# Thirty small DMAs of 1 to 15 rows beside the loads of a one-core attention and gated-MLP decode kernel

## The chip, the cores and the metric

The kernel runs on one NeuronCore of a Trainium2 chip. The metric is the device time of one execution in microseconds. The kernel before took 196.21 us (median of two runs, 196.06 and 196.36). A third execution, taken under the profiler, is the one that every view of the profile below describes.

## The reference

```
W = min(4096, max(256, Sk // 4))                         # 4096 of 16384 cached positions
q = (x @ wq) -> [4 batches, 32 heads, 1, 128]
k = repeat(k_cache[:, :, Sk - W:, :], 4); v the same     # 8 cached heads, 4 query heads to each
p = softmax(q k^T * 128 ** -0.5);  a = (p v) @ wo
gate, up = x @ W_gate, x @ W_up                          # 512 -> 1792
b = (gate * (gate > 0) * up) @ W_down
g = sigmoid(sum(x * gate_w))
out = g * a + (1 - g) * b                                # [4, 1, 512], bf16
```

One token per batch attends to 4096 cached positions of 8 heads. A gated MLP of the same token is mixed in by a scalar gate. Almost all of the work is moving bytes: K and V come to 67 MB, the weights to 14 MB.

## The kernel before

The cache is cut into eight sets (`NSET`), each one half of the heads of one batch. A set's K is one DMA of 4 MB into a half of `Ksb`, and its V one DMA of 4 MB into a half of `Vsb`; both tensors have two halves, so two sets are on the chip at a time. `load_k` (L238) and `load_v` (L242) issue them. The K of set s may be issued when the scores of set s - 2 are done with the half (the event `("SC", s - 2, 3)`), the V when the products of set s - 2 are (`("PV", s - 2, 3)`).

Every large load is issued by SP (SyncE), in the order of the code, on SP's one queue. SP executes in order: a DMA that waits for its event holds up everything behind it. The order is WQ (L248), K of set 0, then for s = 1 to 7 the pair K of s and V of s - 1, then W_gate and W_up (L253, L255) into the half of `Ksb` that is free by then, V of set 7, W_down (L258), and wo in three column pieces (L264) and two last pieces of 128 KB (L267). The output goes out at L600. Only two tiny loads, x of four rows and gate_w of one row, are issued by ACT (L246, L247).

TensorE transposes the K of a set as fp32 pairs into PSUM (L346); ACT and DVE copy the result back over K (L351, L353); TensorE makes scores (L379); DVE masks them and takes maxima (L387); ACT takes exponentials (L416); DVE transposes them (L423); TensorE multiplies with V (L435). The sets s are pipelined: the K of set s is worked on while the softmax and the V product of set s - 1 run. After set 7 come the MLP, and the products with W_down and wo, which add up in one PSUM bank (L572). The very last ones wait for the last 128 KB piece of wo.

Every instruction is recorded in a `Program`, which gives each event a semaphore. `Program.dma` gives each DMA without a slot a semaphore of its own, and a landed DMA adds 16 to it. The last entry of SP's list is a bare wait, emitted behind the block's closing barrier:

```
P.dma("sp", lambda e: e.dma_start(out.rearrange("b o d -> (b o) d"), outs[:, :]), ("OUT",), [("OUTS", 3)])
P.op("sp", None, None, [("OUT",)])
```

Of the kernel before, what the change touches and what calls it, by code (L numbers as in the profile page):

```python
# [6 lines left out]
BF16 = mybir.dt.bfloat16  # L7
# [147 lines left out]
def bass_gated_mix__sliding_block_cached__glu_gated_reglu__decode_kernel(  # L155
# [13 lines left out]
    with ExitStack() as ctx:  # L169
        def sb(name, shape, dt):  # L170
            return ctx.enter_context(nc.sbuf_tensor(name, shape, dt))
# [36 lines left out]
        gtmp2 = sb("gtmp2", [128, NFT, 32], FP32)  # L208
        gtmp3 = sb("gtmp3", [128, NFT, 32], FP32)
        hT = sb("hT", [128, NFT, 32], BF16)  # L210
        outs = sb("outs", [4, 512], BF16)
        banks = [ctx.enter_context(nc.psum_tensor("bank%d" % i, [128, 512], FP32)) for i in range(8)]
        TR = banks[0:NTR]
# [10 lines left out]
        P = Program()  # L224
# [9 lines left out]
        def heads(cache, s):  # L234
            b, half = s // 2, s % 2
            return cache[b, 4 * half:4 * half + 4, SK - WIN:SK, :].rearrange("h (r c) d -> r h (c d)", r=32)

        def load_k(s):  # L238
            P.dma("sp", lambda e: e.dma_start(Ksb[:, s % 2, :], heads(A_k_cache, s)), ("K", s),
                  [("SC", s - 2, NBANK - 1)] if s >= 2 else [], slot="k%d" % (s % 2))  # L240

        def load_v(s):  # L242
            P.dma("sp", lambda e: e.dma_start(Vsb[:, s % 2, :], heads(A_v_cache, s)), ("V", s),
                  [("PV", s - 2, 3)] if s >= 2 else [], slot="v%d" % (s % 2))
# [2 lines left out]
        P.dma("act", lambda e: e.dma_start(xsb[4:5, :], gate_w.rearrange("(o d) -> o d", o=1)), ("GW",))  # L247
        P.dma("sp", lambda e: e.dma_start(Wbig[:, :], A_wq.rearrange("(p t) w -> p (t w)", p=128)), ("WQ",))  # L248
        load_k(0)
        for s in range(1, NSET):  # L250
            load_k(s)
            load_v(s - 1)
        P.dma("sp", lambda e: e.dma_start(Ksb[:, 0, 0:4 * FF], B_W_gate.rearrange("(p t) f -> p (t f)", p=128)),  # L253
              ("WG",), [("SC", NSET - 2, NBANK - 1)])
        P.dma("sp", lambda e: e.dma_start(Ksb[:, 0, 4 * FF:8 * FF], B_W_up.rearrange("(p t) f -> p (t f)", p=128)),  # L255
              ("WU",), [("SC", NSET - 2, NBANK - 1)])
        load_v(NSET - 1)
        P.dma("sp", lambda e: e.dma_start(Vsb[:, 0, 0:NFT * 512], B_W_down.rearrange("(p i) w -> p (i w)", p=128)),  # L258
              ("WD",), [("PV", NSET - 2, 3)])
        wo_src = A_wo.rearrange("(p i) w -> p (i w)", p=128)  # L260
# [337 lines left out]
            else:  # L598
                P.op(engine, lambda e, to=to, src=src: e.tensor_copy(to, src), ("OUTS", g), [("ACC", g)])  # L599
        P.dma("sp", lambda e: e.dma_start(out.rearrange("b o d -> (b o) d"), outs[:, :]), ("OUT",), [("OUTS", 3)])  # L600
        P.op("sp", None, None, [("OUT",)])

        sems = {name: ctx.enter_context(nc.semaphore(name)) for name in P.sems}
        P.emit("sp", nc.sync, sems, 0, 1)
# [50 lines left out]
```

## Time and profile before

| what | value |
|---|---|
| median of the two runs | 196.21 us |
| the profiled execution: its time | 196.31 us |
| its span, first to last instruction | 195.07 us |
| granted TensorE clock, mean | 0.913 |
| PE, DVE, ACT busy | 72%, 55%, 48% of the span |
| POOL busy | 4% of the span |
| instructions of the program on SP | 31 |
| HBM read | 81.01 MB |
| bytes of all DMA packets | 81.17 MB |

The profiled execution took 196.31 us, of which 195.07 us are its span; the 1.24 us around the span are outside the program's own instructions. The page gives the busy time of each engine, and the busy share of the core's 16 DMA engines in 40 slices of the span. The chain of waits is followed back from the last instruction to what released each step. SP's row of the timeline gives the start and the duration of every DMA issue; a gap in it is SP waiting. The page's list of DMA queues gives packets: one packet is what one DMA engine moves in one piece, and each has a start, a duration and a size in the trace. On the queue of the large loads the packets are 32 KB for WQ, K and V, less for the later weights, and 4 bytes for each step that a DMA engine adds to a semaphore. Packets marked "instruction" bring program code.

### The profile page before, as it was taken

How to read it: one execution, taken by the hardware profiler on the slowest of the kernel's cores; microseconds unless marked ns; L12 is line 12 of the kernel's file. 1: busy time of each engine (PE TensorE's matmuls, PEld its weight loads, DVE VectorE, ACT ScalarE, POOL GpSimd, SP SyncE). 2: the span in 40 equal slices, each digit the busy share in tenths (PEclk: the TensorE clock that was granted, in tenths of full speed). 3: DMA queues.
4: the chain of work that ended last, by engine and by line, in shares of the span. 5: the costliest groups of instructions: out<-in, count | busy, mean ns of one | idle time of the engine just before them, and what ended most of it. 6: DMA issues, size and time to landing. Idle time of an engine off the chain costs nothing.

```text
span 195.1 us, 3974 instructions
## 1 busy us (share of the span) xinstructions
PE 139.6 (72%) x1710; PEld 99.7 (51%) x1710; DVE 106.5 (55%) x283; ACT 93.3 (48%) x112; POOL 7.4 (4%) x37
## 2 busy tenths in 40 slices
PE   0135399789499929992999399939992999708665
PEld 0012385446287518751966296628751775404423
DVE  2104055986649455945485648574955595790201
ACT  2002188797088508760786087708860976220001
POOL 7300000000000000000000000000000000000000
PEclk9999999999979996997599859996999699996997
DMA  6999999999999999999999999999999999998992
GB/s 216 430 437 437 430 430 447 430 437 445 440 437 427 437 420 430 425 427 430 430 430 430 430 430 432 430 437 437 430 430 430 437 388 423 472 437 378 431 400 93
DMA packets 3885, 81.17 MB, mean 416 GB/s; under 512 B 409, under 2 KB 930, under 8 KB 1058
## 3 DMA queue, kind: packets, MB, share of 16 engines
q1 hardware_dynamic: 3864, 81.01, 97.2%
q8 instruction: 8, 0.13, 0.3%
q14 instruction: 3, 0.02, 0.0%
q10 hardware_dynamic: 10, 0.01, 0.0%
HBM read 81.01 MB, written 0.00 MB: 415 GB/s over the span
## 4 chain that ended last, share of the span: by engine, by line
DMA 58%; PE 29%; ACT 9%; DVE 1%; issue 1%; SPq 1%
DMA Ksb<-in_A_k_cache_dram 46%; PE bank L346 18%; DMA Wbig<-in_A_wo_dram 12%; ACT Ksb L351 7%; PE bank L379 6%; PE bank L435 2%; PE bank L448 2%; DVE Ksb L353 1%; ACT sc L416 1%; PE bank L572 1%; ACT L416 1%; SPq L264 0%; SPq L248 0%; SPq L258 0%; PE bank L451 0%
## 5 line engine op out<-in xcount | busy, mean ns | idle before, releaser
L346 PE MATMUL bank<-identf,Ksb 128*128 128x128 f32 x512 | 81.6, 314 | 27.4 <-DMA Ksb<-in_A_k_cache_dram 23.4
L351 ACT ACTIVATE Ksb<-bank 128x1024 bf16<-128x1024 bf16 x72 | 71.0, 1023 | 59.4 <-PE bank L346 59.0
L346 PEld LDWEIGHTS bank<-identf,Ksb 128*128 128x128 f32 x512 | 66.8, 161 | 42.1 <-DMA Ksb<-in_A_k_cache_dram 25.2
L353 DVE COPY Ksb<-bank 128x1024 bf16<-128x1024 bf16 x56 | 38.1, 685 | 40.3 <-PE bank L346 39.1
L387 DVE CUSTOM_DVE_ANT_0 sc<-bank,mask 128x512 bf16<-128x512 f32 x32 | 21.7, 686 | 9.7 <-PE bank L379 9.6
L379 PE MATMUL bank<-Ksb,QSP 128*32 128x512 bf16 x256 | 19.8, 390 | 2.2 <-DVE Ksb L353 1.6
L416 ACT ACTIVATE sc<-sc,negmax 128x1024 bf16<-128x1024 bf16 x16 | 18.3, 1145 | 4.8 <-DVE negmax L408 4.7
L423 DVE STREAM_TRANSPOSE pT<-sc 128x1024 bf16<-128x1024 bf16 x16 | 19.7, 1236 | 1.4 <-ACT sc L416 1.2
L435 PE MATMUL bank<-Vsb,pT 128*32 128x256 bf16 x512 | 19.2, 273 | 0.5 <-DMA Vsb<-in_A_v_cache_dram 0.5
L435 PEld LDWEIGHTS bank<-Vsb,pT 128*32 128x32 bf16 x512 | 12.2, 95 | 7.1 <-issue 3.8
L597 ACT ACTIVATE outs<-bank 4x128 bf16<-4x128 f32 x2 | 0.5, 270 | 21.2 <-PE bank L572 21.2
L448 PEld LDWEIGHTS bank<-osb,Wsel 128*64 128x64 f32 x128 | 8.1, 138 | 4.7 <-issue 2.9
L448 PE MATMUL bank<-osb,Wsel 128*64 128x32 f32 x128 | 9.0, 224 | 1.2 <-DVE osb L440 1.2
L516 PE MATMUL bank<-gwB,ident 128*128 128x512 bf16 x14 | 5.4, 535 | 5.4 <-DVE hT L509 5.4
L379 PEld LDWEIGHTS bank<-Ksb,QSP 128*32 128x32 bf16 x256 | 4.1, 94 | 9.6 <-DVE Ksb L353 4.1
L363 POOL COPY QSP<-QS 128x64 bf16<-128x64 bf16 x8 | 1.8, 238 | 119.7 <-PE bank L379 107.6
L440 DVE COPY osb<-bank 128x256 f32<-128x256 f32 x8 | 3.4, 421 | 5.4 <-PE bank L435 5.4
L465 PE MATMUL bank<-Wbig,xP 128*32 128x512 bf16 x32 | 3.6, 631 | 3.6 <-DMA Wbig<-in_A_wq_dram 3.6
L310 PE MATMUL bank<-ident,xsb 5*128 5x5 bf16 x4 | 0.3, 167 | 8.0 <-DMA xsb<-in_gate_w_dram 8.0
L599 DVE CAST outs<-bank 4x128 bf16<-4x128 f32 x2 | 0.6, 282 | 9.6 <-PE bank L572 9.6
L516 PEld LDWEIGHTS bank<-gwB,ident 128*128 128x128 bf16 x14 | 1.4, 118 | 7.7 <-DVE hT L509 5.8
L408 DVE TENSOR_SCALAR negmax<-mall 32x1 f32<-32x1 f32 x32 | 4.6, 144 | 1.0
(61 smaller groups left out, 55.9 us busy)
## 6 DMA issues: line engine op xcount, KB each, us to landing
Ksb<-in_A_k_cache_dram SPq DMA_DIRECT2D x8, 4096.0 KB, 22.7
Vsb<-in_A_v_cache_dram SPq DMA_DIRECT2D x8, 4096.0 KB, 31.9
Wbig<-in_A_wq_dram SPq DMA_DIRECT2D x1, 4096.0 KB, 12.1
Wbig<-in_A_wo_dram SPq DMA_DIRECT2D x1, 2048.0 KB, 20.8
Ksb<-in_B_W_gate_dram SPq DMA_DIRECT2D x1, 1792.0 KB, 18.0
Ksb<-in_B_W_up_dram SPq DMA_DIRECT2D x1, 1792.0 KB, 21.9
Vsb<-in_B_W_down_dram SPq DMA_DIRECT2D x1, 1792.0 KB, 16.3
Wbig<-in_A_wo_dram SPq DMA_DIRECT2D x1, 1280.0 KB, 23.5
```

The costliest lines, as they stand in the source:

```text
L346: P.op("pe", lambda e, bk=bk, cc=cc, c=c, s=s: e.transpose(bk[:, cc * 128:(cc + 1) * 128], kw[:, c * 128:(c + 1) * 128], identf[:, :]), (" ...
L351: P.op("act", lambda e: e.activation(dst, bk[:, :].bitcast(BF16), ACTF.Copy), ("KTC", s, i), [("KT", s, i)])
L353: P.op("dve", lambda e: e.tensor_copy(dst, bk[:, :].bitcast(BF16)), ("KTC", s, i), [("KT", s, i)])
L379: P.op("pe", lambda e, a=a, h=h: e.matmul(bk[32 * a:32 * a + 32, 0:512], QSP[:, s % 2, h, :], k4[:, 16 * bank:16 * bank + 16, 32 * a:32 * ...
L387: P.op("dve", lambda e: e.tensor_tensor_reduce(sc[:, s % 2, bank * 512:(bank + 1) * 512], bk[:, :], mask[:, :], 1.0, LOWEST, ALU.add, ALU.max,
L408: P.op("dve", lambda e, a=a: e.tensor_scalar(negmax[32 * a:32 * a + 32, par:par + 1], mall[:, 0:1], -SCALE, None, op0=ALU.mult), ("NEGMAX" ...
L416: P.op("act", lambda e: e.activation(sc[:, par, k * PW:(k + 1) * PW], sc[:, par, k * PW:(k + 1) * PW], ACTF.Exp, bias=negmax[:, par:par + ...
L423: P.op("dve", lambda e: e.transpose(pT[:, par, k * PW:(k + 1) * PW], sc[:, par, k * PW:(k + 1) * PW]), ("PTT", s, k), [("EXP", s, k), ("PV ...
L435: P.op("pe", lambda e, c=c, g=g, col=col: e.matmul(OB[32 * g:32 * g + 32, 0:256], pT[:, par, col:col + 32], v3[:, 16 * k + c, :], start=(k ...
L448: P.op("pe", lambda e, k=k, lo=lo: e.matmul(FB[r, 256:288], Wsel[:, lo:lo + 64], osb[:, par, 32 * k:32 * k + 32], start=(k == 0), stop=(k ...
L465: P.op("pe", lambda e, n=n, t=t, g=g, j=j: e.matmul(SCB[n][32 * g:32 * g + 32, 0:512], xP[:, t, :], Wq3[:, t, 512 * j:512 * j + 512], star ...
L516: P.op("pe", lambda e: e.matmul(TR[2][:, :], ident[:, :], gwB[:, :], start=True, stop=True), None, waits)
```

## The change

A scratch tensor `probe` is added, 16 partitions of 15 x 2 x 128 bf16 numbers. A function `ask(n, size)` issues 15 DMAs from SP; the k-th moves k rows of 4k + `size` numbers from the first rows of W_gate into `probe`. It is called twice: with size 64 behind the V of set 2, in the loop over the sets (rows of 136 to 248 bytes), and with size 0 behind the V of set 7 (rows of 8 to 120 bytes). No DMA of the two sets waits for anything, nothing reads `probe`, and each of the 30 has a semaphore of its own. The bare wait at the end of SP's list takes in all 30 besides the output's; as it is built, that is 16 semaphore instructions of one or two waits each where there was one, and the output's wait is in the last of them. Nothing changes on the other engines.

```diff
+        probe = sb("probe", [16, 15, 2, 128], BF16)
...
+        def ask(n, size):
+            for k in range(1, 16):
+                P.dma("sp", lambda e, k=k: e.dma_start(probe[0:k, k - 1, n, 0:4 * k + size], B_W_gate[0:k, 0:4 * k + size]),
+                      ("PROBE", n, k))
+
         for s in range(1, NSET):
             load_k(s)
             load_v(s - 1)
+            if s == 3:
+                ask(0, 64)
...
         load_v(NSET - 1)
+        ask(1, 0)
         P.dma("sp", lambda e: e.dma_start(Vsb[:, 0, 0:NFT * 512], B_W_down.rearrange("(p i) w -> p (i w)", p=128)),
               ("WD",), [("PV", NSET - 2, 3)])
...
-        P.op("sp", None, None, [("OUT",)])
+        P.op("sp", None, None, [("PROBE", n, k) for n in range(2) for k in range(1, 16)] + [("OUT",)])
```

## The prediction, made before the changed kernel ran

> **What bounds the kernel now.** First the page's slices, for the DMA engines.
>
> ```profile
> DMA  6999999999999999999999999999999999998992
> GB/s 216 430 437 437 430 430 447 430 437 445 440 437 427 437 420 430 425 427 430 430 430 430 430 430 432 430 437 437 430 430 430 437 388 423 472 437 378 431 400 93
> ...
> q1 hardware_dynamic: 3864, 81.01, 97.2%
> ...
> q14 instruction: 3, 0.02, 0.0%
> ```
>
> From the second slice to the last but three the 16 DMA engines never fall under nine tenths. SP's queue q1 alone fills 97.2% of their span. The kernel is a stream of bytes, and what lengthens the time is what takes DMA time, or what comes behind the stream. Second, the chain of waits over the end:
>
> ```profile
> 167.66 23.46 DMA Wbig<-in_A_wo_dram
> 191.12 0.04 issue
> 191.17 1.91 PE bank L572 x54
> 193.07 0.04 issue
> ```
>
> The last products wait for wo from 167.66 on; in the semaphore records the very last piece lands at 193.07, and 2.0 us of products, copies, output and closing follow. Third, SP's timeline, around the places of the two new sets:
>
> ```profile
> 51.15 0.60 SPq L243 DMA_DIRECT2D Vsb<-in_A_v_cache_dram  x1
> 68.51 0.54 SPq L239 DMA_DIRECT2D Ksb<-in_A_k_cache_dram  x1
> ...
> 147.68 0.55 SPq L243 DMA_DIRECT2D Vsb<-in_A_v_cache_dram  x1
> 166.82 0.33 SPq L258 DMA_DIRECT2D Vsb<-in_B_W_down_dram  x1
> ```
>
> SP idles 16.8 us (51.75 to 68.51) behind the V of set 2, and 18.6 us (148.23 to 166.82) behind the last V. Fourth, the DMA engines alone from 186 us on (40 slices of 0.23 us):
>
> ```profile
> DMA  7986979799799989989966455545000000000000
> ...
> DMA packets 842, 2.10 MB, mean 234 GB/s; under 512 B 76, under 2 KB 592, under 8 KB 720
> ```
>
> The engines do not finish together: from slice 20 (190.6 us) half of them are idle. The 16 steps of the last load's semaphore say it exactly: seven come at 190.91 to 191.19, one at 191.60, seven at 192.37 to 192.67, one at 193.07. The end is set by one DMA engine, 0.40 us behind the next and 2.16 us behind the first. The cause is in the packets: after one 16 KB instruction packet at 31.85, the V of set 0 has 15 steps at 41.70 to 42.04 and one at 43.52.
>
> **The new issues on SP.** One issue takes 0.23 us (gate_w's one row on ACT) to 0.56 us (x's four rows), and 0.04 to 0.06 us lie between two. Fifteen take 4.1 to 9.3 us and end inside SP's 16.8 and 18.6 us. The K of set 4 is queued behind the first set; were the cover gone, it would be issued late, which first costs when q1 runs dry, and the V ahead of it lands only at 80.6 to 82.4. W_down and wo are queued behind the second set; they are issued at 166.8 to 169.6, with the last V landing at 176.6 to 178.8. SP's issues: 0.
>
> **The new packets.** A DMA of k rows makes k packets on k DMA engines and k steps of 4 bytes: x's four rows left four packets and four steps, gate_w's one row one and one. That is 120 packets and 120 steps a set, 0 to 15 of each on an engine. The nearest rows: 512 B takes 27 ns and the next starts 23.5 ns later; 88 B (instruction queue) 9 ns; a 4 B step 9 ns. I take 13 ns for rows of 136 to 248 B (on the line from 88 to 512 B), 9 ns for the second set's 8 to 120 B, and 9 ns a step: 22 + 18 = 40 ns for one of each set. The trace does not show how many fall on the DMA engine that ends last. Half, eight of each set, are 0.32 us. The lower bound is 0 (it gets none). The upper is 15 x 2 x (27 + 9) = 1.08 us. If it gets none and the next one gets all, the end still moves by 0.60 - 0.40 = 0.20. I take 0.32.
>
> The Trainium skill, page "DMA: Bandwidth & Descriptors", section "Why a DMA increments its semaphore by 16 and not by 1", says that such a DMA takes the lowest-numbered k engines, so the first gets 15 of each set and the last none; no view here numbers the engines. By the same page's "Anatomy of one DMA" each DMA has a fixed cost of about 2.0 us (fitted for another issue path); 30 in a row would be 60 us by it, an estimate, against two loads of 128 KB at the end that land 0.36 to 0.40 us apart.
>
> A large packet behind tiny ones may start cold: the first 32 KB packets took 1.59 to 2.15 us, later ones 1.22, so at most 0.93 us a set, 1.9 us in all. No row has a large packet behind small ones. From 16 KB to 512 B packets nothing is lost at a change, so I take 0 and keep 1.9 for the range.
>
> **The new waits.** The 16 semaphore instructions at the end replace one. Now SP leaves the closing barrier at 194.49, and its last wait is recorded at 195.05, because the output's steps come until 195.03. That 0.56 us covers part of the 15 more. SP has no two of them in a row. From SP's own 17 ns of one and the 42 ns between its issues I get 59 ns from one to the next; POOL's pair at the barrier is 78 ns apart, PE's 150 ns. The last starts at 194.49 + 16 x 0.059 = 195.43, 0.38 us later than now; with POOL's 195.74 (+0.69); with PE's 196.89 (+1.84); with 17 ns they hide (0). I take SP's: 0.38. Without the cover it would be 15 x 0.059 = 0.89.
>
> **Sum.** 0 + 0.32 + 0.38 = 0.70. Span 195.07 + 0.70 = 195.77; 1.24 lies around the span, so 197.01. The profiled execution is 0.10 above the median of the runs, so 196.9. The change can hardly gain: even if all DMA engines ended with the first, only 2.16 us would go.
>
> **Rival 1: one more instruction packet.** The three 8 KB packets of q14 come at 44.0, 79.0 and 121.4. By then DVE had started 51 instructions, ACT 52, and DVE 187; POOL, with 47 in all, has none. So an engine seems to get one around its 52nd. SP goes from 31 to 76; its 52nd would be the first wo load, about 167 us. What one costs its DMA engine: 0.5 us (the step at 191.60 fits ACT's one) to 1.0 us (193.07 fits two of DVE's, 2.0 behind). On one of the seven early engines it is hidden; on the last it adds 0.5 to 1.0; on one of the seven late ones 1.0 - 0.40 = 0.6 at most. Time: 197.4 to 197.9. That it comes is likely; that it moves the end by 0.5 or more I give 0.20.
>
> **Rival 2: slower. Each tiny DMA holds its engine until its step is written.** Place: q1 of the first DMA engines, twice 15 steps in a row. Price: from a packet's start to the step seen, 0.36 us (x: 1.76 to 2.12) to 0.45 (192.62 to 193.07). 30 x 0.36 to 0.45 = 10.8 to 13.5 us, less the engine's lead of 0 to 2.16, and 0.38 of waits: 205.2 to 210.1. It makes over 2% from about 0.12 us a DMA (3.9 - 0.38 = 3.5, over 30), or 0.19 with the full lead. For it: no row has steps so close together. Against it: in this slice of the last engine's final packets,
>
> ```profile
> GB/s 0 52 0 0 51 0 51 0 51 0 0 51 0 51 0 51 0 0 51 0 51 0 51 0 0 51 0 51 0 51 0 0 51 0 51 0 0 0 0 0
> DMA packets 17, 0.01 MB, mean 19 GB/s; under 512 B 2, under 2 KB 17, under 8 KB 17
> ```
>
> (192.25 to 192.65) the step of the last load but one is at 192.263, and the next 512 B packet starts at 192.267: 4 ns. Chance 0.06. The page named above, "Queues, rings and completion order", says that a step is written only after every earlier write of its engine; the 4 ns show that the queue does not stand still for that.
>
> **Rival 3: nothing to see.** The late engine gets few of the rows, and SP's semaphore instructions follow at about their own 17 ns, so the output covers them. For it: the rows above leave both open. Against it: POOL and PE take three to five times as long between two as one lasts. Time 196.2 to 196.4. Chance 0.12.
>
> **How the numbers follow.** The forecast has 0.62; its own range is 196.5 (0.2 of packets, few waits shown) to 197.6 (waits by POOL's 0.69 and packets by 0.7). Rivals 0.20, 0.06 and 0.12. The range from 196.2 to 198.2 holds the forecast, rivals 1 and 3, and half of the cold starts; outside are rival 2, the full 1.9 us and PE's pitch together. About 2% (192.3 to 200.1) is what a measurement of this kernel is taken to tell from no change. Faster by that 0.01 (the 2.16 us above are less than 3.9), slower 0.07 (rival 2, and the upper bounds all at once, 196.2 + 1.08 + 1.9 + 1.84 = 201.0), within 0.92.
>
> **What would show it.** SP's timeline: 15 issues behind each of the two Vs, done before 61 and 158 us, the next K and W_down still at about 68.5 and 166.8. Landing steps: the last piece of wo up to 1 us after 193.07, the groups of its 16 steps spread by how many tiny packets each engine got. Packets: tiny ones 10 to 25 ns apart; hundreds of ns would be rival 2. A fourth 8 KB instruction packet near 167 us is rival 1. The end: 16 semaphore instructions on SP some 59 ns apart behind the barrier. I am wrong if the landing of V of set 2 moves by more than 1 us, if q1 shows a gap, or if the end moves by more than the two terms.

## The result, and the profile after

The changed kernel took 199.64 us (median of two runs, 199.57 and 199.72) against 196.21 us: a ratio of 1.0174, 95% interval 1.0158 to 1.0191. It is 3.4 us slower, 1.7%. The forecast was 196.9 us with a range up to 198.2, so the time fell outside it.

The profiled execution took 199.72 us with a span of 198.4 us. The page of the changed kernel, slices of the DMA engines and packets:

```profile
DMA  6999999999999999999999999999999999999981
...
DMA packets 4365, 81.21 MB, mean 409 GB/s; under 512 B 889, under 2 KB 1410, under 8 KB 1538
...
q1 hardware_dynamic: 4344, 81.04, 96.5%
```

The line of packets of the kernel before was:

```profile
DMA packets 3885, 81.17 MB, mean 416 GB/s; under 512 B 409, under 2 KB 930, under 8 KB 1058
```

There are 480 more packets under 512 B than before (889 against 409): the 240 rows and the 240 steps of their semaphores. The stream of bytes has no gap; it is longer. SP's timeline, around the two sets (start, duration, both in us):

```profile
52.33 0.72 SPq L244 DMA_DIRECT2D Vsb<-in_A_v_cache_dram  x1
53.09 5.44 SPq L253 DMA_DIRECT2D probe<-in_B_W_gate_dram  x15
68.49 0.55 SPq L240 DMA_DIRECT2D Ksb<-in_A_k_cache_dram  x1
...
150.43 5.40 SPq L253 DMA_DIRECT2D probe<-in_B_W_gate_dram  x15
169.28 0.35 SPq L267 DMA_DIRECT2D Vsb<-in_B_W_down_dram  x1
169.68 1.38 SPq L273 DMA_DIRECT2D Wbig<-in_A_wo_dram  x3
171.09 4.41 SPq L276 DMA_DIRECT2D Wbig<-in_A_wo_dram  x2
```

Fifteen issues take 5.4 us, inside SP's idle time as forecast; the next K goes out at 68.49, as before (68.51). The chain of waits at the end:

```profile
174.25 21.57 DMA Wbig<-in_A_wo_dram
195.82 0.04 issue
195.86 0.44 PE bank L581 x4
196.31 0.02 issue
196.33 0.27 ACT outs L606
```

The last piece of wo lands at 195.82 instead of 193.07: 2.75 of the 3.41 us between the two profiled executions. The rest, from the semaphore records: the output lands 2.06 us behind that piece (1.96 before), SP's last wait follows 0.48 us later (0.02 before), and 1.34 us lie around the span (1.24 before): 2.75 + 0.10 + 0.46 + 0.10 = 3.41. The DMA engines alone, from 186 us on (40 slices of 0.33 us):

```profile
DMA  9999999997998997798554333213000000000000
```

The engines end between 191.21 (the first step of the last load's semaphore) and 195.82 (the last): a spread of 4.6 us, where it was 2.16. The first is only 0.30 later than before. So the loss is not in all engines alike; some fell far back.

**What held them back.** The first DMA engine takes a packet and a step of each of the 15 DMAs. In the semaphore records of the changed kernel, the steps of the first set that follow each other on that engine come at 80.74, 80.91, 81.09, 81.28, 81.46, 81.66 and so on: 0.17 to 0.20 us apart, though each packet started 18 ns behind the one before. Their data and steps all started by 80.32; the 32 KB packet that started behind them at 80.33 took 2.58 us instead of 1.21. The reading from this, called theory S below: the steps of one DMA engine are written about 0.18 us apart, and a long run of them holds up the large packets behind it. Since the k-th DMA uses k engines, the trace also shows which engine is which: an engine that takes part from the k-th DMA on takes 16 - k of a set. The first step of the second set tells how late each engine was by then (us, relative to the engine that had five steps in the first set; those that had also fetched code are left out):

```
steps in the first set   15    13    11    9     8     7     6     5
lag at the second set    1.55  1.27  1.06  0.95  0.60  0.46  0.07  0
```

Several of the expectations below are worked out from this table: they take a run of n steps to cost n x 0.185 - 1.2 us, so that some six steps are free and fifteen cost 1.5 to 1.6 us. But the engines did not stand level at the first set, and the table leaves that out. A better measure is the time from an engine's first step of the first set to its first step of the second, less the 96.00 us between the first landings of the same two Vs in the kernel before (V of set 2 at 80.55, V of set 7 at 176.55). What the first set cost each engine (us):

```
steps   15    14    13    11    9     8     7     6     5     4     3     2     1
lost    2.00  1.92  1.64  1.41  1.13  1.04  0.46  0.23  0.12  0.10  0.07  0.04  0.03
```

Up to five steps in a row cost 0.12 us or less, six cost 0.23, and fifteen cost 2.0, not 1.55. Two engines are left out: the one with 12 steps lost 2.45 and the one with 10 lost 2.88, and between the two sets one 8 KB and one 16 KB code packet came, which are taken to be theirs.

The engine that ends last can be followed in the same records: its first step of the second set comes with the fourth DMA (180.32), the last at 182.37, the latest of the fifteen that take part. So it is the fourth engine, with 12 of each set. The second ends next. The fourth's loss can be added up: about 1.5 us for the first set, between the 1.41 of 11 steps and the 1.64 of 13, and 1.4 for the second, where its last V step and its W_down step are 5.71 us apart (180.15 and 185.86) against 4.30 before (178.82 and 183.12). This estimate of 2.9 us is near the 2.75 by which the last piece of wo is late.

### The profile page after: what moved, and what is told of

Same layout as the page of the kernel before. It is cut to its first block, busy times and chain, and to the rows that moved or that the text cites. A ratio compares the mean times of both kernels' runs of the same rounds, so it can differ in the third digit from the quotient of the medians.

```text
span 198.4 us, 4016 instructions
## 1 busy us (share of the span) xinstructions
PE 138.2 (70%) x1707; PEld 99.0 (50%) x1710; DVE 106.7 (54%) x283; ACT 93.1 (47%) x112; POOL 7.4 (4%) x37
## 4 chain that ended last, share of the span: by engine, by line
DMA 57%; PE 27%; ACT 8%; DVE 3%; SPq 3%; issue 1%
DMA Ksb<-in_A_k_cache_dram 46%; PE bank L355 17%; DMA Wbig<-in_A_wo_dram 11%; ACT Ksb L360 6%; PE bank L388 5%; PE bank L444 2%; DVE Ksb L362 2%; PE bank L457 2%; SPq L276 2%; ACT sc L425 1%; SPq L273 1%; ACT L425 1%; DVE pT L432 1%; DVE sc L396 0%; PE bank L581 0%
## 5 line engine op out<-in xcount | busy, mean ns | idle before, releaser
L444 PE MATMUL bank<-Vsb,pT 128*32 128x256 bf16 x512 | 19.8, 280 | 0.0
L525 PE MATMUL bank<-gwB,ident 128*128 128x512 bf16 x11 | 4.0, 495 | 6.1 <-DVE hT L518 5.8
L581 PE MATMUL bank<-Wbig,oq 128*32 128x128 bf16 x128 | 2.9, 223 | 4.4 <-DMA Wbig<-in_A_wo_dram 4.4
```

The lines of the kernel that those rows point to most:

```text
L444: P.op("pe", lambda e, c=c, g=g, col=col: e.matmul(OB[32 * g:32 * g + 32, 0:256], pT[:, par, col:col + 32], v3[:, 16 * k + c, :], start=(k ...
L525: P.op("pe", lambda e: e.matmul(TR[2][:, :], ident[:, :], gwB[:, :], start=True, stop=True), None, waits)
```

## The experiments

Each experiment is the changed kernel with the edit shown. Its last wait names the DMAs that it has. The landing of the last piece of wo, from the semaphore records, is called the last piece: 193.07 in the kernel before, 195.82 in the changed one. The ratios are against runs of the kernel before on the same chip, whose medians were 196.24 to 196.34 us.

**Packets kept, steps taken away.**

```diff
-            for k in range(1, 16):
-                P.dma("sp", lambda e, k=k: e.dma_start(probe[0:k, k - 1, n, 0:4 * k + size], B_W_gate[0:k, 0:4 * k + size]),
-                      ("PROBE", n, k))
+            w = 92 if n == 0 else 32
+            rows = B_W_gate[0:15, 0:15 * 112].rearrange("p (k w) -> p k w", k=15)
+            P.dma("sp", lambda e: e.dma_start(probe[0:15, :, n, 0:w], rows[:, :, 0:w]), ("PROBE", n))
```

> Each set is one DMA of 15 rows of 15 pieces: the 15 packets of an engine stay (now on each of 15 engines), but an engine takes one semaphore step a set instead of up to 15, and the end has 2 semaphore instructions instead of 16. Theory S (the steps of one engine land about 0.18 us apart, and a burst holds the stream behind it): the packets alone cost 15 x 15 ns x 2 = 0.45 us on the last engine, so the last piece of wo lands at 193.1 to 193.6 and the time is 196.2 to 196.9. Rival P (tiny packets with their small reads are what costs): all 15 engines now lose as much as the first one did, the last piece lands at 195.5 or later, time 199 or more.

It took 197.58 us, ratio 1.0056 (1.0038 to 1.0073), and the last piece landed at 194.33. That is between the two: above what theory S said, far below the rival's. The page of this kernel:

```profile
DMA packets 4365, 81.22 MB, mean 414 GB/s; under 512 B 889, under 2 KB 1410, under 8 KB 1538
```

It has the very number of small packets that the changed kernel has, 450 pieces and 30 steps instead of 240 rows and 240 steps, and costs 1.2 us instead of 3.4. No large packet behind a set took more than 1.50 us. So the steps are the greater part, but packets are dearer than I had it. The edit takes DMAs away together with their steps, here and in every run below, so a cost of a DMA's end on its engine, other than the writing of the step, is not told apart from the step. The engine that ends first is at 191.65 here (190.91 before): set one delays it by 0.46 us (V of set 2 to V of set 3: 19.89 instead of 19.43), 31 ns for each piece of 184 B; set two by 0.15 (last V to W_down: 4.44 instead of 4.29), 10 ns for each piece of 64 B. That makes 0.6 us of the 0.74 on that engine; why the last engine lost 1.26 is not shown.

**One set alone.**

```diff
-            if s == 3:
-                ask(0, 64)
```

> Only the set behind the last V, 15 DMAs; 8 semaphore instructions at the end. Theory S: a burst of n steps costs its engine n x 0.185 - 1.2 us, so 1.5 for the first engine and 1.4 for the second; these carry up to 1.5 to 2.0 us of lag from code packets, so the last piece lands at 194.1 to 194.6 (193.07 before, 195.82 with both sets), time 197.4 to 198.0. Rival Q (the first set, behind it 100 us of stream, costs the time; the last set comes too late to matter): the last piece within 0.3 of 193.1, time 196.5. Rival Q2 (the last set alone does it): 195.5 or later, time 199.

197.70 us, ratio 1.0063 (1.0046 to 1.0080), the last piece at 194.53, as theory S had it. The second set alone does about half of the harm (1.46 of 2.75 us); it doesn't matter that it comes near the end. The first set was not run alone. The expectation's lag of 1.5 us for the first engine by a code packet was wrong; the kernels with one, three and four rows show which engine is late.

**Fewer semaphores.**

```diff
-        self.event(name, slot or "d_" + "_".join(str(x) for x in name), 16)
+        sem = "d_" + "_".join(str(x) for x in (name[:2] if name[0] == "PROBE" else name))
+        self.event(name, slot or sem, 16)
```

> The same 30 DMAs, but the 15 of a set count on one semaphore, so that 2 semaphore instructions stand at the end instead of 16. Theory S: the steps are as many, so the landing of the last piece stays at 195.8 within 0.3; the end loses the 0.46 us by which SP's last wait came behind the output's landing: 199.2. Rival: steps to different semaphores are what takes 0.18 us apart, and steps to one go faster: the last piece lands before 195, time below 198.6. Rival: the waits hide: 199.6.

199.26 us, ratio 1.0146 (1.0129 to 1.0163), the last piece at 195.97, both as theory S had it. The steps cost the same whether they go to 30 semaphores or to two, and the 14 semaphore instructions that fall away give back 0.38 us. SP's waits at the end, first of the changed kernel, then the wait for the output in the kernel before, then of this one:

```profile
SPq L609 <- ACT outs L606: 21.1, 1, 21.1
SPq L614 <- PEq L614: 0.2, 1, 0.2
```

```profile
SPq L103 <- DMA out_dram<-outs: 0.5, 1, 0.5
```

```profile
SPq L610 <- ACT outs L607: 20.7, 1, 20.7
SPq L104 <- DMA out_dram<-outs: 0.5, 1, 0.5
SPq L615 <- PEq L615: 0.2, 1, 0.2
```

The wait for the output (0.5 us, as in the kernel before) is not in the changed kernel's list: SP was still working through its other waits when the output had landed. With two semaphores the wait is back.

**All steps on one engine.**

```diff
-                P.dma("sp", lambda e, k=k: e.dma_start(probe[0:k, k - 1, n, 0:4 * k + size], B_W_gate[0:k, 0:4 * k + size]),
+                P.dma("sp", lambda e, k=k: e.dma_start(probe[0:1, k - 1, n, 0:4 * k + size], B_W_gate[0:1, 0:4 * k + size]),
```

> All 30 DMAs have one row: 15 packets a set instead of 120, all on one DMA engine, with 15 steps there and none elsewhere. Theory S: that engine loses 1.6 + 1.5 us as before, and lags by a 16 KB code packet too, so the last piece lands at 195.3 to 195.9, time 199.1 to 199.7; of the 16 steps of the last load only one is later than in the kernel before. Rival P (packets or bytes): an eighth of the packets, an eighth of 2.75 us: the last piece at 193.4, time 197.2.

198.89 us, ratio 1.0132 (1.0107 to 1.0156), the last piece at 195.14: 30 rows on one engine do three quarters of the harm that 240 rows on 15 engines do. The last piece is 0.2 us and the time 0.2 us under theory S's range, and that it came so near is luck. By its steps this engine lost 3.9 us in the two sets (2.0 and 1.9) and had no lag, where the expectation had 3.1 us and a lag of 1.5. The DMA engines from 186 us on (40 slices of 0.29 us), in this kernel:

```profile
DMA  9998989989999988664564000000002000000000
GB/s 438 403 473 353 445 353 480 424 353 396 445 424 406 346 297 307 244 258 152 189 203 132 9 28 28 28 28 14 21 21 57 0 0 0 0 0 14 0 0 0
```

From slice 22 (192.4 us) one engine works alone, at 28 GB/s and less, for over 2 us (the 57 in one slice is a 16 KB code packet that starts at 194.89). Fifteen of the last load's steps come from 191.00 to 192.92, the sixteenth at 195.14. The packet records of that engine at the second set say it in small (start in ns, duration in ns, bytes; the middle left out):

```
178457     9      8
178463     9      4
178468     9     16
178474     9      4
...
178643    13    120
178652     9      4
178658  1851  14336
```

All 30 start within 0.2 us, and the 14 KB packet behind them takes 1.85 us where others take 0.54. The 15 steps arrive from 179.14 to 181.71: 0.18 us apart, and the last one 3.1 us behind its start.

**Six DMAs a set instead of fifteen.**

```diff
-            for k in range(1, 16):
-                P.dma("sp", lambda e, k=k: e.dma_start(probe[0:k, k - 1, n, 0:4 * k + size], B_W_gate[0:k, 0:4 * k + size]),
+            for k in range(10, 16):
+                P.dma("sp", lambda e, k=k: e.dma_start(probe[0:15, k - 1, n, 0:4 * k + size], B_W_gate[0:15, 0:4 * k + size]),
```

> Each set is six DMAs of 15 rows, so every one of 15 engines gets six steps a set in place of 1 to 15 (90 packets a set instead of 120); 7 semaphore instructions at the end. Theory S with a free start (a burst costs n x 0.185 - 1.2 us): 6 x 0.185 = 1.1 stays free, only the packets cost, 0.1 to 0.2 us a set: the last piece of wo lands at 193.2 to 193.9, time 196.4 to 197.1. Rival L (each step costs alike, about 0.1 us): 12 steps on every engine, also the one that ends last: 194.3 to 194.8, time 197.6 to 198.1.

197.31 us, ratio 1.0053 (1.0035 to 1.0070), the last piece at 193.94. That is just above theory S (193.9 and 197.1 at most), and below the rival by 0.3 to 0.9 us. The engine that ends first lost 0.43 (191.34), the last 0.87. Six in a row are not quite free: large packets behind the sets took up to 1.71 us instead of 1.21, and up to 1.09 instead of 0.54. By itself this run does not part the two cleanly; the next one does.

**The same DMAs, two at a time.**

```diff
         for s in range(1, NSET):
             load_k(s)
+            ask(2 * s - 1)
             load_v(s - 1)
-            if s == 3:
-                ask(0, 64)
+            ask(2 * s)
...
         load_v(NSET - 1)
-        ask(1, 0)
+        ask(15)
```

Here `ask(k)` issues the k-th DMA of both sets.

> The same 30 DMAs with the same rows, but two behind each of the 15 large loads from the K of set 1 to the last V; all 16 semaphore instructions at the end. Theory S: two steps in a row stay in the free 1.2 us, so the stalls go and only packets are left: the last piece lands at 193.3 to 193.9; with 0.46 for the waits the time is 197.0 to 197.6. Rival L (the cost goes by the number of steps): as with both sets, the last piece at 195.5 or later, time 199.2 or more.

197.58 us, ratio 1.0062 (1.0044 to 1.0080), the last piece at 193.54, as theory S had it. The same 30 DMAs with the same rows and steps now delay the last piece by 0.47 us instead of 2.75, and no large packet behind a set took longer than usual. What costs is the run of steps, not their number.

**Both sets in one run.**

```diff
-            if s == 3:
-                ask(0, 64)
...
+        ask(0, 64)
         ask(1, 0)
```

> Both sets behind the last V, one burst of up to 30 steps on an engine; 16 semaphore instructions at the end. Theory S: the free 1.2 us are there once instead of twice: 30 x 0.185 - 1.2 = 4.35 us on the first engine instead of 2 x 1.55, so the last piece lands about 1.2 us later than in the changed kernel, 196.6 to 197.3, time 200.5 to 201.2. Rival L: as in the changed kernel, 195.8 and 199.6.

200.70 us, ratio 1.0219 (1.0202 to 1.0236), the last piece at 196.93, as theory S had it. With up to 30 steps in a row the free part comes once instead of twice, and the kernel is the slowest of all. This is the counterpart of the run before: same DMAs, worse placed.

**Larger rows.**

```diff
-        probe = sb("probe", [16, 15, 2, 128], BF16)
+        probe = sb("probe", [16, 1024], BF16)
...
-                P.dma("sp", lambda e, k=k: e.dma_start(probe[0:k, k - 1, n, 0:4 * k + size], B_W_gate[0:k, 0:4 * k + size]),
+                P.dma("sp", lambda e, k=k: e.dma_start(probe[k:k + 1, :], B_W_gate[k:k + 1, 0:1024]),
...
-            if s == 3:
-                ask(0, 64)
```

> One set behind the last V, 15 DMAs of one row of 2048 bytes each, all on the first DMA engine; 8 semaphore instructions at the end. It settles what the 0.18 us from step to step are. Theory S1 (a step goes out when the write of its own data is confirmed; the data's own time comes on top): steps 0.24 to 0.28 us apart, as a 4096-byte packet takes 0.16. Theory S2 (the step itself holds the write side 0.18 us, and data goes beside it): still 0.18 apart, and the first engine's loss is 1.5 as with tiny rows. The last piece lands at 193.9 to 194.7 (S1) or 193.1 to 193.9 (S2), by how far that engine lags already.

196.61 us, ratio 1.0015 (1.0006 to 1.0025), the last piece at 193.58. The first four gaps between steps are 0.22 to 0.30 us, the other ten 0.17 to 0.20, though each row's packet takes 84 ns or more (the last six 92 to 174). The first four are as S1 had it. The other ten are as S2 had it: there 0.18 us is a time of the step, and the data passes beside it. The last piece is 0.75 us later than with fifteen tiny rows on the same engine (192.83, next); many 14 KB packets, more than one engine moves in this time, took 0.6 to 0.84 us instead of 0.54 here, and why is not shown.

**The burst on the first engine, behind and ahead of the last V.** The edits are those of the one-row kernel and of the one-set kernel together. In the second, the set is moved as well:

```diff
+        ask(1, 0)
         load_v(NSET - 1)
-        ask(1, 0)
```

> 15 one-row DMAs behind the last V alone, all on the first DMA engine; 8 semaphore instructions at the end. Packets of 32 KB (1.21 us) stand before the burst, of 14 KB (0.54 us) behind it. Theory S: that engine loses 1.3 us (half of what it lost with both sets of one-row DMAs) beside the 1.5 us of a code packet, so the last piece lands at 193.6 to 194.0, time 196.9 to 197.4. The large packet behind the burst takes 1.8 instead of 0.54 us.

> The same 15 one-row DMAs, ahead of the last V, behind W_up: now 14 KB packets (0.54 us) stand before the burst and 32 KB packets behind it. It asks what the free 1.2 us are. Theory F (a fixed lead of the read side, in time): the same loss of 1.3 us, the large packet behind the burst takes 1.2 + 1.3 = 2.5 us, the last piece at 193.6 to 194.0, time 196.9 to 197.4. Theory G (the one large packet before the burst, whose write is still under way): 0.54 is free instead of 1.21, the loss is 2.0 us, the packet takes 3.2 us, the last piece at 194.3 to 194.7, time 197.6 to 198.1.

They took 196.25 us, ratio 0.9999 (0.9989 to 1.0008), and 196.32 us, ratio 1.0002 (0.9992 to 1.0012). Both expectations for the time failed, and that told most. The large packet behind the burst took 1.85 us in the one and 2.53 in the other, as expected (theory F; G's 3.2 is out). The one after it was longer by 0.5 too. With the burst's own 0.2 us, the first engine lost about 2.0 us, where the expectation had 1.3. Yet the last piece landed at 192.83 and 192.94. I had thought that the first engine also fetches code and lags by 1.5 us; it does not. It came out level with the late engines, and a whole burst cost nothing.

**Three rows and four rows.** So a burst should cost time only on an engine that is late already. One set, behind the last V; the edit for three rows, with 4 in place of 3 for four:

```diff
-                P.dma("sp", lambda e, k=k: e.dma_start(probe[0:k, k - 1, n, 0:4 * k + size], B_W_gate[0:k, 0:4 * k + size]),
+                P.dma("sp", lambda e, k=k: e.dma_start(probe[0:3, k - 1, n, 0:4 * k + size], B_W_gate[0:3, 0:4 * k + size]),
```

> 15 DMAs of three rows behind the last V: 15 steps on each of the first three DMA engines. By the small rows of the changed kernel's trace, the second engine already lags 1.1 us by a code packet at that point, the first and the third none, and the fourth 2.0; the fourth gets nothing here. Theory D (only the engine that ends last counts, each engine by its own steps): the first and third come to 2.0 behind and stay hidden, the second to 2.5 to 3.1: the last piece at 193.5 to 194.1, time 196.7 to 197.3. Rival (three times the packets of the one-row kernel cost three times as much, wherever they fall; that one cost 0.0): no change, 193.1 and 196.3.

> The same with four rows: the fourth DMA engine, which lags 2.0 us by two code packets, now gets 15 steps too. Theory D: it comes to 4.0 behind the first to end, so the last piece lands at 194.8 to 195.2, time 198.0 to 198.5, 1.0 us or more above three rows. Rival (cost by the number of packets or steps in all): a third more than three rows, under 0.4 us above it.

Three rows: 196.83 us, ratio 1.0024 (1.0014 to 1.0034), the last piece at 193.70. Four rows: 198.31 us, ratio 1.0107 (1.0090 to 1.0124), the last piece at 194.97. The DMA engines of the four-row kernel from 186 us on (40 slices of 0.30 us):

```profile
DMA  9989998979899898766752100000200000000000
GB/s 423 430 369 416 430 430 341 498 300 485 375 410 386 309 340 331 307 246 207 242 171 82 55 29 27 17 20 22 63 0 0 0 0 0 7 7 0 0 0 0
```

One engine is alone again from slice 23 (192.9 us) to the end; the steps of the last load are at 191.02 to 193.37, and 194.97. One more row in each DMA, on the fourth engine, makes 1.5 us; the first row made none, the next two 0.6. That the fourth was late before its burst stands in the steps: the first ones of the set come at 177.07, 177.15 and 177.76 on the three engines, and at 176.94, 176.99, 177.45 and 178.93 on the four. So the fourth is 2.0 us behind, as expected, but of the first three none lags by more than 0.7, where 1.1 was expected of the second: how late an engine is differs from kernel to kernel.

## Why the prediction was wrong

**What bounds the kernel: right.** The time moved with the landing of the last piece of wo, and that is set by one DMA engine. One reading was off by a slice: the last slice but three stands at eight tenths, not at nine.

**The issues on SP: right.** 5.4 us each, inside the idle time, at no cost.

**The new packets: wrong, 0.32 forecast, 2.75 measured.** This is the step that failed, in two places. First the price. I took 40 ns for one packet and step of each set, from how soon the next packet starts. That the next packet starts 4 ns behind a step is true here too (5 or 6 ns in the rows above), and says nothing of when the step is written: the step that started at 192.263 was seen at 192.71. The row that I used against rival 2, the end of the stream, has two steps 0.36 us apart with 16 packets between them; at 0.18 us a step nothing can pile up there. The records of steps, not of packets, would have been the place to look, and no row of the kernel before has steps closer together than that. Second the engine. I gave the last engine half of the rows because the trace did not number the engines; it is the fourth, with 12 of 15, as the three- and four-row kernels show. The price is what failed most: 12 of each set at my 40 ns make 0.48 us, and even the upper bound of the prediction, 15 of each, was 1.08. The Trainium skill, page "DMA: Bandwidth & Descriptors", section "Why a DMA increments its semaphore by 16 and not by 1", has the lowest-numbered engines take such a DMA; the traces agree, as each longer DMA adds one engine to the same ones.

**Rival 2: the right mechanism, the wrong price and form.** Each step does take time of its own, 0.18 us where I had 0.36 to 0.45, some five in a row cost almost nothing, and the engine that ends last takes 12 of a set and not 15, so it gave 199.6 and not 205. I gave it 0.06. The same page of the Trainium skill, section "Anatomy of one DMA", calls the step's own write "essentially free", in a part on another issue path. For one or two steps the traces agree (0.03 to 0.04 us lost in the first set), for a run of fifteen they do not (2.0).

**The cold large packet: taken at 0, and nearly so.** Behind the one-step sets, with as many small packets, no 32 KB packet took over 1.50 us (1.21 elsewhere) and no 14 KB packet over 0.69 (0.54), so up to 0.3 us each. The long ones (2.58) come with the steps.

**The new waits: right in kind, a little small.** 0.38 forecast; SP's 16 instructions came 60 ns apart (59 forecast), the last 0.48 us behind the output (0.02 before), and taking 14 of them away gave 0.38 us. In the profiled executions the whole way from the last piece to the end is 3.24 us before, 3.24 to 3.35 in the kernels with two to eight of these instructions, and 3.88 to 4.00 in the four with 16.

**Rival 1: wrong in its premise.** No fourth 8 KB code packet came in the span (one came at 199.69, behind the end), though SP passed its 52nd instruction at 169 us. But code packets seem to have decided where the steps hurt.

## What to carry to other kernels

A DMA costs its engine more than its bytes: the semaphore step at its end. A few between large loads cost next to nothing (30 DMAs, two at a time, set back the last piece by 0.47 us); fifteen in a row on one engine set back the loads behind them by about 2.0 us. Put small transfers into one DMA, or place them two at a time between large ones, and ask on which engines they fall: with few rows they all fall on the same few, and whether that costs anything depends on whether one of these is the one that ends last.

## What the runs showed of the hardware that was not expected

- Steps that follow each other on one DMA engine are written about 0.18 us apart (0.16 to 0.24 over all engines of the changed kernel), for rows of 8 bytes as, from the fifth gap on, of 2 KB, to one semaphore as to fifteen. What in the write path takes this time, and why some five in a row cost so little, stays open; that the free part does not go by the size of the packet ahead is shown (0.54 or 1.21 us ahead, the same loss).
- SP's issue itself can stall: the last two loads of wo took 3.12 and 1.25 us to issue with the second set still queued, 0.44 and 0.47 before. It cost nothing, as the stream was 20 us behind. Too many DMAs under way would explain it, and the other runs agree. The two issues took 4.4 to 6.9 us in all in every other kernel with one set of fifteen queued, also with one row each. They took 0.95 where one, two or six were queued, or where the fifteen were queued ahead of the last V and landing by then. With 30 queued the stall came earlier: the three pieces of wo took 8.60 us instead of 1.38. Which queue was full is not shown.
- Code packets seem to make DMA engines unequal. In the changed kernel the second, fourth and sixth engine were 1.2, 2.0 and 1.5 us later at the second set than their steps explain. The second had its lag at the first set already, the fourth half of it, the sixth none. Between the sets came one 16 KB code packet at 88.73 (0.96 us) and one 8 KB packet at 121.50 (0.32 us), and the 32 KB packets behind them took 1.76 and 1.87 us instead of 1.21: 1.5 and 1.0 us in all, about what the sixth and the fourth lost there. That the fourth's two 8 KB packets are DVE's code is inferred from their times, not shown.
